# Seven half-size products for the last block's output projection, in a newly searched order

## The chip, the cores and the metric

The kernel runs on one core of one Trainium2 chip. Its engines work side by side, each through its own list of instructions in order: TensorE (PE, its weight loads shown as PEld), VectorE (DVE), ScalarE (ACT), GpSimd (POOL) and SyncE (SP). They wait for each other by semaphores. DMAs are issued here from POOL (loads, which also turn f32 into bf16) and from SP (stores and DMA transposes), and run on the same 16 DMA engines. The metric is the device time of one execution in microseconds, the median of several runs.

## The reference

```python
k_proj = np.einsum('ks,bhsd->bhkd', E, k)
v_proj = np.einsum('ks,bhsd->bhkd', F, v)
scores = scale * np.matmul(q, k_proj.transpose(0, 1, 3, 2))
attn = softmax(scores)                                   # over the 64 projected keys
x = np.matmul(attn, v_proj)   ->  x of 8192 tokens x 512
out = ((1 / (1 + np.exp(-(x @ w_gate)))) * (x @ w_val)) @ w_out
```

Eight batches, eight heads, 1024 positions, head size 64: attention against 64 projected keys, and then a gated feed-forward layer with d_model 512 and d_ff 1536. Inputs and output are f32; the kernel multiplies in bf16.

## The kernel before, in words

A batch gives two blocks of 512 tokens, so there are 16 blocks. For each batch, attention makes `xT` (x transposed, in bf16) for its two blocks: POOL loads K, V and Q in halves of four heads (512 KB each in SBUF); TensorE projects K and V (job `kv`); SP turns Q by DMA transposes (`turnq`, four per batch) and the projected K (`turnk`); TensorE makes the scores (`sc`), DVE the row maxima and their subtraction, ACT the exponentials; SP turns these (`turnp`); TensorE multiplies with V (`xo`); DVE inverts the sums, POOL or DVE divides; SP turns the result (`turnx`). K and V share SBUF with the exponentials and the quotients, so the loads of a batch wait until the previous one's `turnx` transposes have landed.

Then each block goes through the feed-forward layer. The gate product G and the value product V have a 2x2 split (half of the 512 inputs by half of the 1536 hidden units, two halves of the tokens) that is computed with seven half-size products instead of eight (`seven`, L1152). Sums of quarters are formed first: S1 = A21 + A22, S2 = S1 - A11, S3 = A11 - A21, S4 = A12 - S2 (`xs_sum`), and sums of the weights T1 to T4. The seven are A11·B11, A12·B21, S2·T2, S1·T1, S3·T3, A22·T4 and S4·B22. They accumulate in three PSUM banks a, c and f: ACT copies a to c after the first; copies a out ("snap") after S2·T2 and again after S3·T3; DVE adds a copy to f. One such product is four matmuls of 256 columns.

The output projection is done by `o_jobs` (L1369). For the first block and the last, it is plain (`o_plain`, L1309): for each of four tiles of 128 tokens, 12 matmuls of 512 columns into a bank, a copy by ACT and a store of 256 KB; in the last block the fourth tile is cut into two halves of 256 columns, with two stores of 128 KB. For the 14 blocks between, it is the same seven-product scheme, each product in two pieces j of six matmuls with 256 columns (0.65 us), with the sums S1 to S4 of the hidden units formed by `s_sum` (L1251; S4 on POOL in the middle blocks, where `AT["g4"]` is 1). There DVE merges f with a copy of a (`mergeO`), ACT copies c and a out (`leaveO`), and four stores follow.

All work outside the constants is cut into jobs, numbered in the order of their creation. `ORDER` (L159) lists these numbers in the order in which the instructions are put out; each engine takes its own of them in that order. A -1 stands for one fill product (`busy`, L720): a matmul of 256 columns with the unit matrix, whose result nobody reads. `PLACES` (L315) gives each job's PSUM bank or buffer. `Scheduler.job` (L350) takes a `release` argument and does not keep it.

Jobs that the texts speak of: 0 and 1, 6 and 7 are the products of the first K projection; 2, 3, 8, 9 copy it; 12, 14, 32, 34 transpose Q; 4 and 10 transpose K; 16, 22, 36, 42 are scores (17, 23, 37, 43 their maxima); 28, 30, 48, 50 transpose the exponentials; 52, 53, 59, 60 project V; 56, 63 make x; 112 to 163 are plain products of the first block, the first two of after's list being 119 and 113. Batch 1: 294 and 301 project K and V, 306 to 309 are its `turnq`. Batch 4: 1017 to 1020 load K and V, 1021 and 1022 Q, 1023 to 1026 are `turnq`, 1027 is `kv`, 1030 `turnk`. Batch 6: 1753 loads the first half of K, 1754 to 1756 the rest of K and V, 1763 is `kv`; 2014 to 2016 are S4 sums of an output block, 1904 and 1906 sums of x for S2 and S4. Near the end: 2850 is the last value product, 2851 its addition, 2820, 2847, 2849 and 2852 are gates, 2873 to 2882 belong to block 14's output, and 2887 on is the last block's output (before 15 jobs to 2901, in after 32 jobs to 2918: 2887 to 2892 the sums S1 to S3, 2893/2894 A11·B11, 2895 the bank copy, 2896/2897 A12·B21, 2898 S4, 2899 copy of c, 2900/2901 S2·T2, 2902 copy of a, 2903/2904 S1·T1, 2905/2906 A21·T3, 2907 copy, 2908 merge, 2909/2910 A22·T4, 2911 copy, 2912/2913 A12·B22, 2914 merge, 2915 to 2918 the stores).

Of the kernel before, what the change touches and what calls it, by code (L numbers as in the profile page):

```python
# [29 lines left out]
    s2=0, s3=0, s4=0, s5=0, s6=0, s7=0, o0p=1, o1p=0, o2p=0, o3p=1, x1=0, x2=0, x3=0, x4=1, g1=0, g2=0, g3=0,  # L30
# [123 lines left out]
class Job:  # L154
# [221 lines left out]
def bass_linformer_attn__then__ffn_glu_sigmoid_kernel(  # L376
# [20 lines left out]
    with contextlib.ExitStack() as es:  # L397
# [383 lines left out]


        def first_batch():
            K_AT, Q_AT = ((6.4, 8.05), (10.65, 12.0)), ((9.35, 13.4), (28.8, 30.1))
            V_AT = ((15.9, 15.9), (18.35, 19.45))
            ENGS = ("ACT", "DVE", "POOL")

# [1117 lines left out]
```

## Time and profile before

| | us |
|---|---|
| median of 3 runs (517.63 to 518.54) | 518.26 |
| the profiled execution's own time | 518.57 |
| its span, first to last instruction | 516.8 |
| TensorE busy | 510.5 (99%) |
| DVE busy | 436.6 (84%) |
| ACT busy | 374.4 (72%) |
| POOL busy | 169.8 (33%) |

The page cuts the span into 40 slices of 12.9 us: the busy digit of TensorE is 9 in all but the first and the last, and so is the granted clock in all. The 16 DMA engines are busy at nine tenths in the first five slices and move 138 GB/s on the mean. A group line gives an operation's shape, its count, the busy time and the mean of one. Matmuls are pipelined, so the time that one adds is the step from its start to that of the next, not its shown duration. "Idle before" and the waits name what ended an engine's wait.

### The profile page before, as it was taken

How to read it: one execution, taken by the hardware profiler on the slowest of the kernel's cores; microseconds unless marked ns; L12 is line 12 of the kernel's file. 1: busy time of each engine (PE TensorE's matmuls, PEld its weight loads, DVE VectorE, ACT ScalarE, POOL GpSimd, SP SyncE). 2: the span in 40 equal slices, each digit the busy share in tenths (PEclk: the TensorE clock that was granted, in tenths of full speed). 3: DMA queues.
4: the chain of work that ended last, by engine and by line, in shares of the span. 5: the costliest groups of instructions: out<-in, count | busy, mean ns of one | idle time of the engine just before them, and what ended most of it. 6: DMA issues, size and time to landing. Idle time of an engine off the chain costs nothing.

```text
span 516.8 us, 12171 instructions
## 1 busy us (share of the span) xinstructions
PE 510.5 (99%) x4741; PEld 426.6 (83%) x4741; DVE 436.6 (84%) x849; ACT 374.4 (72%) x714; POOL 169.8 (33%) x196
## 2 busy tenths in 40 slices
PE   8999999999999999999999999999999999999997
PEld 4555867889988899888998888888998889988884
DVE  6769998699988899869997799978989889968771
ACT  1566956888876796767867789777878679686652
POOL 9882004520435033340245113620053502403020
PEclk9999999999999999999999999999999999999999
DMA  9999938896679946995579957796545994530204
GB/s 159 198 198 207 181 70 175 136 201 124 148 148 170 188 92 128 155 179 115 119 143 174 158 103 128 156 196 113 142 98 129 202 169 104 96 90 1 82 2 162
DMA packets 140521, 71.57 MB, mean 138 GB/s; under 512 B 97200, under 2 KB 132272, under 8 KB 140464
## 3 DMA queue, kind: packets, MB, share of 16 engines
q1 hardware_dynamic: 104560, 40.91, 37.8%
q0 software_dynamic: 35904, 29.89, 37.8%
q8 instruction: 37, 0.61, 0.5%
q14 instruction: 20, 0.16, 0.1%
HBM read 60.29 MB, written 16.78 MB: 149 GB/s over the span
## 4 chain that ended last, share of the span: by engine, by line
PE 55%; DMA 3%; issue 1%; POOL 1%; ACT 0%; POOLq 0%
PE pF L518 28%; PE pA L518 27%; DMA KVs<-in_k_dram 3%; POOL KVs L559 0%; POOL Qb L559 0%; ACT ost L532 0%; POOL xS L547 0%; POOLq L129 0%
## 5 line engine op out<-in xcount | busy, mean ns | idle before, releaser
L532 ACT ACTIVATE spare<-pF 128x512 f32<-128x512 f32 (+2 forms) x167 | 94.2, 574 | 32.0 <-PE pF L518 22.7
L547 POOL TENSOR_TENSOR hT<-hT,hS 128x512 bf16<-128x512 bf16 x42 | 48.1, 1164 | 174.2 <-PE pA L518 96.8
L532 ACT ACTIVATE spare<-pA 128x512 f32<-128x512 f32 (+2 forms) x146 | 83.7, 586 | 20.2 <-PE pA L518 16.3
L1724 POOL TENSOR_TENSOR KVs<-spare,inv 128x384 bf16<-128x384 f32 (+1 forms) x41 | 29.6, 731 | 84.4 <-DVE topf L1635 35.3
L532 ACT ACTIVATE spare<-spare 128x512 f32<-128x512 f32 x74 | 46.1, 628 | 5.9 <-DVE spare L1146 5.5
L1146 DVE TENSOR_TENSOR spare<-pF,spare 128x512 f32<-128x512 f32 x59 | 40.1, 681 | 10.5 <-PE pF L518 5.2
L1215 DVE SCALAR_TENSOR_TENSOR hT<-spare,pF 128x512 bf16<-128x512 f32 x60 | 40.8, 679 | 7.7 <-PE pF L518 3.7
L518 PE MATMUL pA<-wO,hT 128*128 128x256 bf16 (+1 forms) x336 | 47.2, 280 | 0.0
L1146 DVE TENSOR_TENSOR spare<-pA,spare 128x512 f32<-128x512 f32 x54 | 36.7, 681 | 8.8 <-PE pA L518 6.4
L1215 DVE SCALAR_TENSOR_TENSOR hT<-spare,pA 128x512 bf16<-128x512 f32 x52 | 35.3, 678 | 8.3 <-PE pF L518 4.1
L518 PE MATMUL pF<-wO,hT 128*128 128x256 bf16 (+1 forms) x276 | 42.2, 296 | 0.0
L518 PE MATMUL pF<-xT,wV 128*128 128x256 bf16 (+1 forms) x248 | 39.9, 283 | 0.0
L518 PEld LDWEIGHTS pA<-wO,hT 128*128 128x128 bf16 x336 | 32.8, 98 | 6.5 <-ACT KVs L532 0.2
L518 PE MATMUL pA<-xS,wV 128*128 128x256 bf16 x248 | 37.2, 273 | 0.0
L518 PE MATMUL pA<-xT,wG 128*128 128x256 bf16 (+1 forms) x220 | 35.4, 284 | 0.6 <-DVE xT L876 0.5
L518 PE MATMUL pF<-xS,wG 128*128 128x256 bf16 x232 | 34.1, 272 | 0.0
L518 PEld LDWEIGHTS pF<-wO,hT 128*128 128x128 bf16 x276 | 26.6, 98 | 8.7
L518 PE MATMUL pF<-xS,tV 128*128 128x256 bf16 x224 | 33.6, 273 | 0.0
L518 PE MATMUL pA<-xS,tG 128*128 128x256 bf16 x208 | 31.2, 273 | 0.0
L518 PE MATMUL pF<-xT,wG 128*128 128x256 bf16 (+1 forms) x188 | 30.9, 286 | 0.0
L532 ACT ACTIVATE EF<-pA 128x512 f32<-128x512 f32 (+2 forms) x35 | 19.7, 564 | 14.4 <-PE pA L518 13.5
L518 PEld LDWEIGHTS pF<-xT,wV 128*128 128x128 bf16 x248 | 23.9, 98 | 4.3
(186 smaller groups left out, 1288.7 us busy)
## 6 DMA issues: line engine op xcount, KB each, us to landing
out_dram<-ost SPq DMA_DIRECT2D x63, 256.0 KB, 2.4
KVs<-in_v_dram POOLq DMA_DIRECT2D x15, 512.0 KB, 9.4
KVs<-in_k_dram POOLq DMA_DIRECT2D x14, 512.0 KB, 10.2
Qb<-in_q_dram POOLq DMA_DIRECT2D x14, 512.0 KB, 8.8
wO<-in_moe_w_out_dram POOLq DMA_DIRECT2D x1, 1536.0 KB, 28.1
wG<-in_moe_w_gate_dram POOLq DMA_DIRECT2D x5, 256.0 KB, 16.9
wV<-in_moe_w_val_dram POOLq DMA_DIRECT2D x5, 256.0 KB, 17.3
KVs<-in_k_dram POOLq DMA_DIRECT2D x4, 256.0 KB, 6.8
```

The lines of the kernel that those rows point to most:

```text
L518: lambda e: e.matmul(o, lhsT, rhs, **kw),
L532: lambda e: e.activation(o, i, func, scale=scale),
L547: fn = lambda e: e.tensor_tensor(o, a, b, op)
L1146: lambda e: e.tensor_tensor(PB(b)[:, :] if stay else BF(s), PB(b)[:, :], BF(s), ALU.add),
L1215: lambda e: e.scalar_tensor_tensor(o, y.rearrange("p (j c) -> p j c", j=2), 1.0, x.rearrange("p (j c) -> p j c", j=2), ALU.add, ALU.mult,),
L1724: fn = lambda e: e.tensor_tensor(xto.rearrange("p (g h d) -> p h g d", g=2, h=H)[:, hh[0] : hh[1], :, :], o[:, :, 0:DH].rearrange("p (h g) ...
```

## The change

`AT["o3p"]` goes from 1 to 0, so that `o_jobs` sends the last block through the seven-product scheme instead of `o_plain`. For that block all four sums are on DVE (`s_jobs` takes POOL only for blocks 1 to 14). `ORDER` and `PLACES` are new as a whole: all jobs are in a new order with new banks and buffers, and the list has 54 fill products instead of 35. The constants `K_AT`, `Q_AT`, `V_AT` and `LAND`, which go into `release`, are new. The order was searched with a longer share of the DMA engines given to the transposes. Everything else stays. Of the diff, the parts with the start, the loads and transposes of batch 4, batch 6's loads, and the end (in before's list, 1753 to 1757 stand together):

```diff
@@ -27,7 +27,7 @@
...
-    s2=0, s3=0, s4=0, s5=0, s6=0, s7=0, o0p=1, o1p=0, o2p=0, o3p=1, x1=0, x2=0, x3=0, x4=1, g1=0, g2=0, g3=0,
+    s2=0, s3=0, s4=0, s5=0, s6=0, s7=0, o0p=1, o1p=0, o2p=0, o3p=0, x1=0, x2=0, x3=0, x4=1, g1=0, g2=0, g3=0,
...
@@ -157,188 +157,189 @@
...
 ORDER = (
-    0, -1, -1, -1, 1, 2, -1, -1, -1, -1, -1, -1, 14, 3, -1, 4, 15, 12, 5, -1, 6, 13, -1, 16, 22, 17, -1, 7, 23,
-    18, 19, 8, -1, -1, -1, 24, 34, 9, 20, 25, -1, -1, 10, 32, 35, 11, 21, 33, 26, -1, -1, -1, -1, -1, -1, -1,
-    -1, -1, 36, 42, 28, 37, 52, 43, 38, 53, 39, 27, 44, 54, 29, -1, 30, 45, 40, 59, 55, 31, 46, -1, -1, -1, -1,
-    -1, 56, 41, 60, 57, 47, 48, 58, 169, 61, -1, -1, 50, 49, 119, 62, 168, 51, 112, 346, 63, 118, 174, 64, 65,
-    113, 124, 176, 128, 126, 125, 180, 130, 129, 127, 178, 114, 131, 115, 116, 165, 120, 68, 175, 122, 66, 121,
...
-    1267, 1188, 1242, 1176, 1269, 1189, 1243, 1178, 1022, 1099, 1191, 1179, 1282, 1036, 1100, 1192, 1182, 1190,
-    1252, 1246, 1019, 1271, 1183, 1194, 1247, 1167, 1020, 1241, 1195, 1255, 1244, 1018, 1193, 1256, 1169, 1198,
-    1017, 1253, 1199, 1258, 1177, 1259, 1248, 1180, 1262, 1026, 1254, 1203, 1276, 1196, 1204, 1025, 1184, 1263,
-    1181, 1205, 1197, 1257, 1206, 1283, 1249, 1219, 1260, 1284, 1277, 1185, 1220, 1200, 1245, 1278, 1207, 1201,
...
-    1421, 1217, 1027, 1231, 1422, 1261, 1410, 1024, 1213, 1228, 1288, 1502, 1028, 1229, 1423, 1029, 1425, 1506,
...
-    1976, 1989, 1757, 2005, 1913, 1992, 1756, 1835, 1978, 2011, 1994, 1916, 1979, 1754, 2018, 1820, 1990, 1753,
...
-    1951, 2022, 2142, 1962, 2238, 2143, 1904, 1952, 1937, 1906, 2144, 1961, 1963, 1938, 2024, 1905, 1966, 2157,
-    1967, 2145, 1933, 1763, 2146, 1953, 2025, 2240, 2158, 2242, 1954, 2026, 2159, 1764, 1964, 2148, 2030, 1765,
...
-    2832, 2808, 2845, 2868, 2833, 2783, 2843, 2801, 2863, 2846, 2810, 2871, 2772, 2865, 2867, 2827, 2848, 2864,
-    2850, 2849, 2869, 2787, 2866, 2812, 2870, 2830, 2872, 2788, 2831, 2834, 2795, 2813, 2873, 2798, 2874, 2847,
-    2811, 2851, 2875, 2816, 2799, 2814, 2877, 2876, 2818, 2815, 2802, 2880, 2817, 2878, 2803, 2881, 2835, 2879,
-    2819, 2893, 2804, 2883, 2836, 2882, 2884, 2820, 2885, 2886, 2852, 2887, 2890, 2888, 2894, 2896, 2891, 2892,
-    2899, 2889, 2897, 2898, 2895, 2900, 2901,
+    0, -1, -1, -1, -1, -1, -1, 1, 2, 3, -1, -1, -1, -1, -1, -1, -1, 12, -1, 4, 13, 14, 15, -1, -1, -1, 6, 5, -1,
+    22, 16, 23, -1, 7, 24, 8, 17, 9, -1, -1, -1, -1, 32, 34, 25, -1, 18, 33, 10, 26, 19, 35, 11, 20, -1, -1, -1,
+    -1, -1, -1, -1, -1, -1, -1, -1, -1, 42, 36, 52, 43, 27, -1, -1, 44, 45, 37, -1, -1, -1, 30, 21, -1, -1, -1,
+    38, 53, 39, 46, 28, 31, 59, 29, 54, 40, 55, -1, -1, -1, -1, -1, -1, -1, 56, 47, 60, 57, 41, 50, 58, 169, 61,
+    -1, -1, -1, 48, 51, 119, 168, 49, 62, 113, 63, 174, 118, 64, 65, 112, 346, 121, 128, 175, 120, 114, 176,
...
+    1246, 1020, 1099, 1179, 1164, 1251, 1190, 1192, 1018, 1182, 1247, 1282, 1019, 1252, 1194, 1084, 1253, 1017,
...
+    1280, 1193, 1199, 1259, 1248, 1257, 1022, 1249, 1262, 1278, 1196, 1177, 1219, 1263, 1207, 1180, 1220, 1200,
...
+    1406, 1214, 1228, 1216, 1215, 1407, 1217, 1409, 1231, 1421, 1027, 1222, 1026, 1422, 1410, 1213, 1025, 1229,
+    1285, 1028, 1286, 1029, 1288, 1501, 1408, 1030, 1423, 1502, 1289, 1232, 1169, 1031, 1290, 1425, 1023, 1412,
+    1218, 1503, 1411, 1413, 1233, 1294, 1426, 1024, 1506, 1416, 1234, 1428, 1417, 1505, 1291, 1032, 1414, 1427,
...
+    1943, 1996, 2014, 1941, 1944, 2008, 1984, 1942, 1927, 1755, 1985, 1946, 1928, 1906, 2000, 1947, 1929, 2001,
+    1986, 1955, 2015, 2017, 1950, 2002, 1956, 1930, 2007, 1945, 1753, 1931, 1957, 1948, 1951, 1757, 2141, 1917,
...
+    2024, 1963, 1905, 2021, 2025, 1953, 2022, 1964, 1936, 2026, 2143, 1965, 1966, 1763, 1937, 1967, 1759, 1997,
...
+    2772, 2846, 2801, 2827, 2856, 2812, 2787, 2863, 2813, 2788, 2795, 2866, 2848, 2830, 2811, 2798, 2834, 2865,
+    2868, 2814, 2799, 2849, 2831, 2816, 2864, 2869, 2867, 2817, 2871, 2835, 2870, 2872, 2847, 2818, 2888, 2802,
+    2819, 2873, 2890, 2874, 2815, 2850, 2803, 2875, 2893, 2836, 2876, 2877, 2804, 2851, 2880, 2820, 2894, 2887,
+    2881, 2895, 2852, 2878, 2892, 2889, 2896, 2879, 2882, 2900, 2891, 2885, 2901, 2884, 2903, 2883, 2902, 2886,
+    2905, 2906, 2897, 2907, 2904, 2898, 2909, 2908, 2910, 2912, 2911, 2913, 2899, 2915, 2916, 2914, 2917, 2918,
...
@@ -781,8 +782,8 @@
 
 
         def first_batch():
-            K_AT, Q_AT = ((6.4, 8.05), (10.65, 12.0)), ((9.35, 13.4), (28.8, 30.1))
-            V_AT = ((15.9, 15.9), (18.35, 19.45))
+            K_AT, Q_AT = ((7.05, 8.4), (11.1, 12.45)), ((9.8, 13.75), (29.1, 30.45))
+            V_AT = ((16.35, 16.35), (17.7, 20.3))
             ENGS = ("ACT", "DVE", "POOL")
 
             def step(name, key, n, body, keep, release=0.0):
@@ -1009,8 +1010,8 @@
             )
 
         LAND = {
-            "G": (20.1, 21.45, 26.1, 34.2, 23.5, 31.5, 36.85),
-            "V": (20.75, 22.15, 27.5, 35.5, 24.8, 32.9, 38.25),
+            "G": (20.5, 21.75, 26.4, 34.65, 23.75, 32.1, 37.3),
+            "V": (21.05, 22.45, 27.8, 36.0, 25.05, 33.35, 38.7),
         }
 
         def landed(n, j):
```

325 rows, old and new, of tables (ORDER, PLACES) are left out of this document.

## The prediction

> **What bounds the kernel now.** I read four views, in this order: the waits of TensorE, the busy time by stretch, the chain around the one long wait, and the timeline of both ends. The waits of TensorE (engine, line, releaser: total us, times, longest):
>
> ```profile
> PE pA L518 <- DMA KVs<-in_k_dram: 1.1, 2, 0.9
> PE pA L518 <- DVE tV L642: 1.1, 1, 1.1
> PE pA L518 <- DVE xT L876: 0.5, 1, 0.5
> ```
>
> Little else waits. The busy time by stretch (window: length, then PE, PEld, DVE, ACT, POOL busy, granted clock, DMA share, GB/s):
>
> ```profile
> 24.00:62.00 38.00, 37.34 (x300) 23.58 (x299) 32.41 (x63) 26.27 (x51) 16.63 (x17) 1.00 1.32 201
> 62.00:200.00 138.00, 138.00 (x1300) 116.96 (x1301) 122.88 (x241) 107.30 (x207) 41.33 (x48) 1.00 0.80 144
> 200.00:240.00 40.00, 39.12 (x361) 34.32 (x359) 33.54 (x61) 29.16 (x56) 13.16 (x15) 1.00 0.91 150
> 240.00:500.00 260.00, 260.00 (x2497) 229.98 (x2495) 223.79 (x424) 198.31 (x380) 77.65 (x85) 1.00 0.62 122
> ```
>
> TensorE is full outside three places: the start, 24 to 62 us and 200 to 240 us. So the time moves by TensorE work added or removed, by its few waits, and by the tail. The chain from 205 to 235 us (start, length, what) shows the long wait:
>
> ```profile
> 210.43 0.81 POOL Qb L559
> ...
> 212.36 2.25 POOL KVs L559 x3
> 214.61 16.57 DMA KVs<-in_k_dram
> 231.17 0.04 issue
> 231.22 1.99 PE pA L518 x16
> ```
>
> A half of K for batch 4 needs 16.57 us to land. The trace's landings show why: a half of Q was loaded first (landed 216.74), and two Q transposes ran through the four K and V loads, which landed 3.0 to 4.1 us apart (220.86, 224.85, 227.88, 231.17). One batch later, with no transpose among them, they landed 2.5 to 2.8 us apart. The timeline of the end (start, length, engine, line, out<-in):
>
> ```profile
> 503.56 5.34 PE L518 MATMUL pF<-wO,hT 128*128 128x512 bf16 x24
> 508.74 2.75 PE L518 MATMUL pA<-wO,hT 128*128 128x512 bf16 x12
> 511.33 1.47 PE L518 MATMUL pF<-wO,hT 128*128 128x256 bf16 x12
> 512.64 1.47 PE L518 MATMUL pA<-wO,hT 128*128 128x256 bf16 x12
> 514.15 0.38 ACT L532 ACTIVATE ost<-pA 128x256 f32<-128x256 f32 x1 [0.87 <-PE pA L518]
> 514.56 0.33 SPq L1360 DMA_DIRECT2D out_dram<-ost  x1
> ```
>
> The plain block runs without a gap; then one small copy and one half-size store remain (landed 516.30).
>
> **The change, part by part.** The sum is against the profiled execution: span 516.8, time 518.57, so 1.77 lies around the span. The median of the runs, 518.26, is 0.31 lower, and I carry the difference over to it.
>
> *Start.* The list of after has 54 fill products (-1) where before has 35, all ahead of the plain products. Fills here step by 0.109 us (nine from 15.05 take 1.0), so 19 more are 2.07 us. Part of it fills waits: by the step from each matmul to the next, before loses about 1.6 us between 7.5 and 22.2 us. I walked the new order by hand with durations of the timeline: score reduce or normalize on DVE 0.59 a step, sum with reciprocal 0.82, exp 0.60, a bank's turned copy 0.34 on DVE and 0.5 to 0.6 on ACT, 0.43 from a product's start to its reader. The loads of the start are issued as before, so they land as before (K 8.41, 11.10, 12.43). The first K product moves from 8.48 to 8.82, the last from 12.47 to 12.7, first scores of the second four heads from 16.16 to 16.27. DVE then has idle bits of 0.8 us that before hasn't, its last two normalizations end at 22.35 (before 21.6), and three fills stand between the last two transposes: the first plain product starts at 23.07, not 22.22. **+0.85**; from 0 (the fills replace waits only) to 2.07 (none hidden). I take the walk, whose durations are rows of this stretch.
>
> *22 to 62 us.* Before has small waits here: 0.34 in all at 22.4 to 24.3, 0.19 at 30.05 (Q landed 30.41), 0.25 at 34.4 (a gate weight landed 34.64) and, from step to step, 0.70 at 48.2 (the profile's 0.5, ended by DVE's copy of xT). In after's order the products that need those loads stand 1 to 5 us behind the landings, and a plain product and the V projection stand between the copy and the first products that need its sums. **-1.48**; 0 if equal waits come back. Batch 1's K is loaded before both Q halves (by the bytes ahead of it landing near 56.5, not 58.99); its Q transposes begin near 59.0 instead of 56.50, but its first scores come near 67, and need two that I expect by 65.6.
>
> *Batch 4.* The Q half that led is now behind the K and V loads, and the transposes stand behind the projection on SP. The loads should land near 226, the projection stands at 227 to 231. **-1.05** (the step from 230.06 is 1.156, an undisturbed one 0.107); between 0 and that.
>
> *Last block.* Plain: 503.56 to 513.95 (the last row plus twelve steps) is 10.39 us. Seven products of 12 matmuls, 84 by 0.1093 (that last dozen's step): 9.18. **-1.21**. Six sums by DVE for S1 to S3 (0.41 at 512 elements, 0.68 at 1024), one for S4 (near 0.95, extrapolated), two copies to spare, a bank copy and two merges are new. Most lie beside: after the last value product DVE still has a sum-and-gate tail of 3.6 us, but four pieces of block 14's products and both first pieces of A11 (0.655 each) cover it. Not covered: the copy of bank a between S2·T2 and A21·T3 takes 0.91 from the end of one to the start of the other (as 499.15 to 500.06), with one piece of 0.655 between: 0.25, and 0.05 for the sum S2 being just late. **+0.3** (0.25 if the sum is on time, 0.9 if DVE is one 0.6 step late).
>
> *Tail.* Before, from the last matmul's slot (513.95) to the landing: 0.2 + 0.38 copy + 0.03 + 1.74 = 2.35. After: 0.25, then the last merge on DVE 0.68, 0.03, one store issue of 0.40, then the second 256 KB store. SP issues them in order behind the other two, ready 1.4 us earlier, so these don't block. A lone store landed in 2.03 to 2.06, the fourth in a row in 2.56; two behind two is between, 2.25. Together 3.6: **+1.25** (1.0 to 1.6). The Trainium skill, DMA: Bandwidth & Descriptors, section "Anatomy of one DMA — SWDGE (gpsimd) path", fits a fixed 2.0 us plus bytes over 436 GB/s, for another issue path: an estimate of 2.6 us for the last store, and of 517.55 for the run. The trace's lone stores are faster.
>
> *New waits elsewhere.* Every other step is reordered too; counts of all other instructions stay. From 62 to 500 us before has one long wait, and otherwise about 0.3. Copy-to-product distances in after's list are as short as before's, but one is shorter: a sum, a gate and a bank copy ahead of a value product near 106 have about 0.3 us too little. The landing constants in the diff enter only an argument that Scheduler.job drops: no instruction. **+0.3** by the nearest row; below nothing only by the waits already taken out, and at most 2.6 if waits of before's size return.
>
> Sum: 0.85 - 1.48 - 1.05 - 1.21 + 0.3 + 1.25 + 0.3 = **-1.04**, so 517.2 against the median.
>
> **The rivals.**
> *The fills are not covered* (start +2.07): 517.2 + 1.22 = 518.4. For it: TensorE does 0.86 us more work in all. Against it: 1.6 us of waits at the start.
> *Transposes meet loads elsewhere*: 1.05 comes back, 518.25, at worst 519.2. For it: in batch 7 before already waits 0.15 at 425.8 on the K transpose, behind three Q transposes on SP, and after has 7.1 us of TensorE work from projection to score against 8.4. Against it: loads start earlier there. The Trainium skill, DMA: Bandwidth & Descriptors, "Queues, rings and completion order", says that each engine takes turns between the queues that have work; by that a transpose in flight slows every load, as the 3.0 to 4.1 us spacing above agrees.
> *Slower: batch 6's K half is late.* On POOL that load now stands behind two S4 sums and one x sum (1.16 to 1.39 each), with 7.4 us of TensorE work from its place to the projection. A load alone lands 5.6 us after issue, behind another 8.2. POOL waited 4.18 us for DVE before such an x sum at 350.61; if it does so here, the landing is 9.8 to 12.4 after the place, a wait of 2.4 to 5.0, and 519.6 to 522.2. It makes the kernel slower by 0.2% from a wait of 2.1 us on, that is 3.9 us of delay. Against it: the sums that it waits for stand 3.3 us ahead.
> *The start costs nothing* (fills only replace waits): 516.3.
>
> **How the numbers follow.** 0.2% (1.04 us) is about what a measurement can tell. Forecast 0.50, own range 516.4 to 518.0: it lies at the bound, and since the terms above it are waits seen and those below are priced by rows, I give 0.34 faster, 0.16 within. Fills 0.14 (0.12 within, 0.02 slower); transposes 0.14 (0.10 within, 0.04 slower); the late K half and its like 0.12, slower; the cheap start 0.10, faster. Faster 0.44, within 0.38, slower 0.18. The range 516.2 to 519.4 leaves out the worst of the late load and the best of the cheap start.
>
> **What would show it.** First plain product near 23.1; no wait near 48 and at batch 4's projection; the last product block near 9.5 us with one gap of 0.25 after S2·T2; 3.6 us from the last matmul to the last landing; 62 to 500 us full. It is wrong if a KVs or kpD landing ends a wait over 1 us, or the first plain product comes after 24.

## The result, and the profile after

The kernel became slower: 520.45 us (median of 9 runs, 519.93 to 523.05) against 518.26 (9 runs beside them), a ratio over all runs of 1.0051 with a 95% interval of 1.0036 to 1.0066 (the two medians alone give 1.0042). That is 1.9 to 3.4 us more, where the prediction had 1.0 less and its range ended at 519.4. The profiled execution took 520.57 with a span of 518.7, 2.00 more than the one of before (518.57).

The waits of TensorE, in the changed kernel (engine, line, releaser: total us, times, longest; line numbers are one higher than before):

```profile
PE pA L519 <- DVE tV L643: 1.1, 1, 1.1
PE pA L519 <- issue: 0.7, 1, 0.7
PE pF L519 <- DMA KVs<-in_k_dram: 0.4, 1, 0.4
PE pF L519 <- ACT pF L533: 0.3, 1, 0.3
PE pA L519 <- DMA Qb<-in_q_dram: 0.3, 1, 0.3
PE pF L519 <- ACT spare L533: 0.2, 1, 0.2
```

The 0.9 us of batch 4's K load and the 0.5 of the copy of xT, which the change was to remove, are gone. The other 0.2 of before's 1.1 for K loads belong to the first K load of the start, and are 0.4 now. Three new releasers stand in their place, and one wait of 0.7 with the releaser "issue", that is, none that the profile can name.

The busy time by stretch, changed kernel, same windows and columns as for before:

```profile
24.00:62.00 38.00, 37.34 (x305) 23.71 (x304) 31.31 (x62) 26.75 (x51) 17.24 (x18) 1.00 1.31 199
62.00:200.00 138.00, 137.11 (x1284) 115.54 (x1283) 121.89 (x235) 105.33 (x204) 41.35 (x48) 1.00 0.75 142
200.00:240.00 40.00, 40.00 (x374) 34.68 (x373) 34.00 (x66) 29.68 (x57) 13.38 (x16) 1.00 0.90 161
240.00:500.00 260.00, 260.00 (x2494) 229.48 (x2492) 226.43 (x428) 197.56 (x381) 76.51 (x85) 1.00 0.63 122
```

200 to 240 us is full now, as predicted. But 24 to 62 us has lost just as much as before (37.34 of 38.00 in both), and 62 to 200 us, which was full, has lost 0.9. The chain through the place where K was late for 1.05 us has no gap in it any more (start, length, what):

```profile
229.32 1.31 PE pF L519 x12
230.63 0.44 PE pA L519 x4
231.06 1.85 PE pF L519 x16
```

The timeline of the end (start, length, engine, line, out<-in):

```profile
512.95 1.47 PE L519 MATMUL pF<-wO,hT 128*128 128x256 bf16 x12
...
513.86 2.27 SPq L1303 DMA_DIRECT2D out_dram<-ost  x4
514.56 0.69 DVE L1405 SCALAR_TENSOR_TENSOR ost<-pF,spare 128x512 f32<-128x512 f32 x1 [1.75 <-PE pF L519]
```

The last slot of TensorE ends at 514.26, only 0.31 later than before. Then comes the merge on VectorE, which only begins when the last product is done, and two whole stores behind it, issued at 515.32 and 515.70; the last landed at 517.95, 3.69 us after the last slot, against 2.35 before.

Read matmul by matmul (the step from one to the next, less the usual step of its size), the places where TensorE lost over 0.15 us between 22 and 93 us are:

| before, at us | lost | changed, at us | lost | what ends it in the changed kernel |
|---|---|---|---|---|
| 22.0, 24.2 | 0.34 | 24.98 | 0.19 | no releaser named; before's at 24.2 is as long and stands at the same weight half |
| 30.05 | 0.19 | 29.05 | 0.46 | Q's third part, landed 29.67 |
| 34.4 | 0.25 | 56.48 | 0.50 | ScalarE's copy of a bank |
| 48.2 | 0.70 | 80.50 | 0.23 | ScalarE's copy out of a bank of products with V |
| | | 90.78 | 0.88 | the second transpose of the attention output, landed 91.69 |
| sum | 1.48 | sum | 2.26 | |

At 69.63 and 77.06 us the step is 0.22 too long as well, but no wait lies there: the trace lacks the record of a matmul. The weight loads go on at their usual step, the profile counts 312 weight loads and 310 matmuls with wO into pF, and early_after, mid_after and plain_end below, which have the same order there, show no such step. They also make some 0.1 of the 0.9 that the busy time lacks from 62 to 200 us. The recorded expectations below count them as waits: their 2.70 should be 2.26, and the price of the early order in them 0.80 + 0.78, or 1.6, and not 2.0.

The copy that ends the wait at 56.48 stands on ScalarE directly behind another operation that ended at 56.43 (start, length, engine, line, out<-in):

```profile
56.46 0.58 ACT L533 ACTIVATE pF<-pF 128x512 f32<-128x512 f32 x1
```

So most of the early waits went, but others came, and more of them.

### The profile page after: what moved, and what is told of

Same layout as the page of the kernel before. It is cut to its first block, busy times and chain, and to the rows that moved or that the text cites. A ratio compares the mean times of both kernels' runs of the same rounds, so it can differ in the third digit from the quotient of the medians.

```text
span 518.7 us, 12271 instructions
## 1 busy us (share of the span) xinstructions
PE 511.1 (99%) x4782; PEld 429.7 (83%) x4784; DVE 441.6 (85%) x858; ACT 372.8 (72%) x714; POOL 168.7 (33%) x196
## 4 chain that ended last, share of the span: by engine, by line
PE 90%; DMA 3%; DVE 3%; POOL 2%; issue 0%; ACT 0%; DVEq 0%; ACTq 0%; POOLq 0%
PE pA L519 45%; PE pF L519 45%; DMA Qb<-in_q_dram 3%; POOL KVs L560 1%; DVE topf L1636 1%; POOL wG L560 1%; POOL wV L560 1%; DVE pF L1663 0%; DVE pA L1663 0%; DVE hT L1216 0%; POOL Qb L560 0%; DVE hS L548 0%; ACT spare L533 0%; DVE ost L1405 0%; DVE hT L1057 0%
## 5 line engine op out<-in xcount | busy, mean ns | idle before, releaser
L533 ACT ACTIVATE spare<-pF 128x512 f32<-128x512 f32 (+2 forms) x152 | 86.1, 577 | 37.1 <-PE pF L519 27.1
L533 ACT ACTIVATE spare<-pA 128x512 f32<-128x512 f32 (+2 forms) x167 | 92.2, 572 | 27.3 <-PE pA L519 15.2
L1725 POOL TENSOR_TENSOR KVs<-spare,inv 128x384 bf16<-128x384 f32 (+1 forms) x52 | 37.5, 730 | 104.2 <-DVE topf L1636 36.4
L519 PE MATMUL pA<-wO,hT 128*128 128x256 bf16 (+1 forms) x276 | 37.9, 277 | 0.1
L519 PE MATMUL pA<-xT,wV 128*128 128x256 bf16 (+1 forms) x212 | 34.2, 285 | 0.0
L519 PE MATMUL pF<-xT,wV 128*128 128x256 bf16 (+1 forms) x196 | 32.0, 286 | 0.0
L519 PE MATMUL pF<-xS,wV 128*128 128x256 bf16 x208 | 31.0, 272 | 0.0
L519 PEld LDWEIGHTS pA<-wO,hT 128*128 128x128 bf16 x276 | 26.4, 98 | 4.4 <-ACT spare L533 0.2
L519 PE MATMUL pF<-wT,hT 128*128 128x256 bf16 x216 | 28.5, 273 | 0.2 <-ACT spare L533 0.2
L519 PE MATMUL pF<-xS,tV 128*128 128x256 bf16 x184 | 27.1, 273 | 0.0
```

The source lines that it names most:

```text
L519: lambda e: e.matmul(o, lhsT, rhs, **kw),
L533: lambda e: e.activation(o, i, func, scale=scale),
L1725: fn = lambda e: e.tensor_tensor(xto.rearrange("p (g h d) -> p h g d", g=2, h=H)[:, hh[0] : hh[1], :, :], o[:, :, 0:DH].rearrange("p (h g) ...
```

## The experiments

The change has four parts in time: the start to 23 us, the stretch to 93 us, the rest of the middle (batch 4 with it), and the last block. A given job number is the same job in both lists up to 2886, and at any time each list has at most 11 jobs behind it that the other has still ahead, so one can follow one list to a point and the other one from there on. In all kernels of this kind the banks and buffers of the second list are renamed where needed, so that none is held twice. Ratios are to the kernel before on the same chip; times worked out from them are on its 518.26. My theory after the traces was that the early order costs 2.0 (1.6 without the two missing records), batch 4 gains 1.05 and the last block loses 0.5 to 0.8; the rival, that the early order is worth what was predicted and the last block costs it all.

**Early order alone, and everything but it.**

```diff
 ORDER = (
-    0, -1, -1, -1, 1, 2, -1, -1, -1, -1, -1, -1, 14, 3, -1, 4, 15, 12, 5, -1, 6, 13, -1, 16, 22, 17, -1, 7, 23,
...
+    0, -1, -1, -1, -1, -1, -1, 1, 2, 3, -1, -1, -1, -1, -1, -1, -1, 12, -1, 4, 13, 14, 15, -1, -1, -1, 6, 5, -1,
...
+    519, 504, 435, 434, 556, 501, 436, 542, 502, 517,
     439, 520, 518, 437, 440, 522, 557, 505, 438, 400,
```

> The kernel before, with only its first 443 jobs (to about 93 us, the fills of the start included) in the order of the changed kernel; the rest, batch 4's loads and the plain last block too, in the old order. Theory (the lost time lies in the early order): the start costs 0.80 and the waits from 24 to 92 us are 2.70 against 1.48, so 518.26 + 2.0 = 520.3. Rival (the early order is worth what the prediction said, +0.85 - 1.48, and the loss comes from the end): 517.6.

Measured: 1.0037 (1.0023 to 1.0051), that is +1.9 us (1.2 to 2.6). The other half, against the changed kernel:

```diff
 ORDER = (
-    0, -1, -1, -1, -1, -1, -1, 1, 2, 3, -1, -1, -1, -1, -1, -1, -1, 12, -1, 4, 13, 14, 15, -1, -1, -1, 6, 5, -1,
...
+    0, -1, -1, -1, 1, 2, -1, -1, -1, -1, -1, -1, 14, 3, -1, 4, 15, 12, 5, -1, 6, 13, -1, 16, 22, 17, -1, 7, 23,
...
+    440, 522, 557, 505,
     523, 400, 506, 554, 399,
```

> The changed kernel with its first 458 jobs in the old order: the 35 fills and the stretch to about 93 us are those of the kernel before, all that follows is new, the seven products at the end too. Theory (early order): 520.45 - 2.0 = 518.4. Rival (loss at the end): 520.45 + 0.6 = 521.1.

Measured: 1.0004 (0.9995 to 1.0014), +0.2 (-0.3 to +0.7), 518.5 on the base of before. Both agree with the theory, with 1.6 as with 2.0 for the early order, and both exclude the rival: nearly all of what the whole change loses is in its first 93 us. The two make 2.1 together, inside the 1.9 to 3.4 of the whole.

**The start and the stretch behind it, apart.** Both lists have the same 61 jobs ahead of the first plain product, so they can be cut there.

```diff
 start_after:
...
+    -1, -1, -1, 48,
     49, 119, 62, 168, 51, 112, 346, 63, 118, 174, 64, 65,
 mid_after:
     61, -1, -1, 50,
+    51, 119, 168, 49, 62, 113, 63, 174, 118, 64, 65, 112, 346,
...
```

> The kernel before with only its first 61 jobs (all ahead of the first plain product) and the 54 fills in the new order. Theory (the prediction's walk): the first plain product starts 0.80 to 0.85 later and everything behind it too, 519.1. Rival (all 19 more fills count): 520.3. Rival (the later start only takes the place of the waits for loads at 24, 30 and 34 us, 0.78 in all): 518.3.

Measured: 1.0003 (0.9989 to 1.0017), +0.2 (-0.6 to +0.9). The interval has both the +0.85 of the walk and nothing; it excludes that all 19 fills count. In its profiled execution the first plain product stands at 23.26, 1.0 later than before's, and the waits from 22 to 62 us are 1.07 instead of 1.48: part of the later start is taken back because the loads are then there. That execution is among its longest (519.62): a sum on VectorE at 210.41 took 2.38 us instead of 0.68, beside a sum of GpSimd's, and TensorE lost 1.03 waiting for it at 211.71. I don't take more from it.

> The kernel before with its own start (35 fills, 61 jobs), then the jobs to about 93 us (the next 382) in the new order, then the old order again. Theory (the waits that went have come back as others): 2.70 against 1.48 between 22 and 93 us, +1.2, 519.5. Rival (the prediction's two terms, -1.48 and +0.3): 517.1.

Measured: 1.0017 (1.0002 to 1.0032), +0.9 (0.1 to 1.7). The prediction's two terms for this stretch (-1.48 and +0.3, 517.1) are excluded. With the start's +0.2 that makes 1.1, against 1.9 for the two together; the intervals cover the difference, and say no more of it. The waits of this kernel:

```profile
PE pA L517 <- DMA Qb<-in_q_dram: 0.9, 1, 0.9
PE pA L517 <- issue: 0.8, 1, 0.8
...
PE pF L517 <- ACT pF L531: 0.3, 1, 0.3
```

The reader is to see that the same three come back that the changed kernel has, at 28.28, 90.58 and 56.28 us. With the shorter start the first is larger (1.02 by the step): Q's third part landed at 29.47, and the new order has its product 1.0 us earlier than that.

**Batch 4 alone.**

```diff
-    1178, 1022, 1099, 1191,
+    1178, 1099, 1191,
...
-    1198, 1017, 1253,
+    1198, 1017, 1022, 1253,
...
-    1262, 1026, 1254, 1203, 1276, 1196, 1204, 1025, 1184,
+    1262, 1254, 1203, 1276, 1196, 1204, 1184,
...
-    1217, 1027, 1231,
+    1217, 1027, 1026, 1025, 1231,
```

> The kernel before with three jobs moved: batch 4's first half of Q is loaded behind its four K and V loads instead of ahead of them, and the two Q transposes stand behind the K projection instead of ahead of it. Theory: the wait of 1.05 (1.2 and 1.4 in two of the runs above) goes and nothing takes its place, 518.26 - 1.05 = 517.2. Rival (the Q transposes are then late for the first scores, or meet other loads): 518.3.

Measured: 0.9981 (0.9969 to 0.9993), -1.0 (-1.6 to -0.4), as predicted for this step. The four loads landed 2.5 to 3.2 us apart (216.78, 219.39, 221.93, 225.15), before 3.0 to 4.1 apart with the last at 231.17; the stretch by busy time is full:

```profile
200.00:240.00 40.00, 40.00 (x370) 34.66 (x369) 34.25 (x62) 29.56 (x56) 13.16 (x15) 1.00 0.93 152
```

**One early wait removed by hand.** At 48 us before waits for a copy on VectorE that stands behind two weight sums and a gate. Here it is put ahead of them.

```diff
-    187, 192, 109, 185, 302, 143, 198, 110, 214, 111, 199, 182,
+    187, 109, 111, 192, 185, 302, 143, 198, 110, 214, 199, 182,
```

> As the last one, and at 48 us the copy of the attention output (VectorE) stands directly behind the product that it reads, ahead of two weight sums and one gate that stood before it. Theory: the wait of 0.70 at 48.2 us goes as well, 516.5 to 516.7. Rival (the weight sums are now late for the first products that use them): 517.2.

Measured: 0.9979 (0.9969 to 0.9990), no different from the last one. The rival's time holds (no gain, 517.2), though what is late is a sum of x and not a weight sum; the timeline shows it (start, length, engine, line, out<-in, idle before and its releaser):

```profile
47.21 0.69 DVE L875 CAST xT<-pA 128x512 bf16<-128x512 f32 x1
...
48.31 1.04 PE L517 MATMUL pA<-xT,wG 128*128 128x256 bf16 x8
...
50.09 0.42 DVE L546 TENSOR_TENSOR xS<-xS,xT 128x512 bf16<-128x512 bf16 x1
...
50.56 0.61 PE L517 MATMUL pA<-xS,tG 128*128 128x256 bf16 x4 [0.79 <-DVE xS L546]
```

The copy ends 1.0 us earlier and its products run without a gap. One product group later TensorE waits 0.79 for a sum of the same x (a step 0.95 over the usual one), because VectorE, which is idle for under 0.2 us between 46 and 51 us, does the same work in another order. Here the wait for a full engine was not removed by letting its work change places; one such move was tried.

**The last block alone.**

```diff
     2774, 2679, 2673, 2677,
-    2680, 2748, 2854, ..., 2898, 2895, 2900, 2901,
+    2748, 2746, 2762, ..., 2914, 2917, 2918,
```

> The kernel before with only its last 180 jobs replaced: old order to about 480 us, then the new order with the last block in seven products. Theory: products -1.21, the gap for the bank copy +0.35, the tail from the last matmul to the landing +1.34: +0.5, 518.7; up to 519.0 when what lies behind the last landing is longer too. Rival (the end is what costs the 2.2): 520.4. Rival of the change's own: the products' saving is not eaten by the tail, 517.3.

Measured: 1.0010 (0.9998 to 1.0021), +0.5 (-0.1 to +1.1), as the theory has it and not clear of nothing; 520.4 and 517.3, the two rivals, are both out. The products pay 1.21, and the gap and the longer tail eat it.

```diff
-    2878, 2892, 2889, 2896, ..., 2913, 2899, 2915, 2916, 2914, 2917, 2918,
+    2878, 2879, 2882, 2885, 2884, 2883, 2886,
+    2893, 2887, 2890, 2888, 2894, 2896, 2891, 2892, 2899, 2889, 2897, 2898, 2895, 2900, 2901,
```

> The changed kernel with the last block's plain products put back at the end of its order (54 fills and all of the new order kept). Theory: 520.45 - 0.5 to 0.8, 519.65 to 519.95. Rival (the end costs the 2.2): 518.3. If the seven products do pay by themselves: 521.0 or more.

Measured: 1.0026 (1.0014 to 1.0039), so 519.6 on the base of before, as the theory has it. Some of the difference to the changed kernel is given away here: two pieces of A11 B11 stood among block 14's products; without them TensorE waits 0.42 at 501.5 and 0.15 at 502.6, where the changed kernel has no wait.

**The last block with a shorter tail.**

```diff
-    2892, 2889, 2896, 2879, 2882, 2900, 2891, 2885, 2901, 2884, 2903, 2883, 2902, 2886, 2905, 2906, 2897, 2907, 2904,
-    2898, 2909, 2908, 2910, 2912, 2911, 2913, 2899, 2915, 2916, 2914, 2917, 2918,
+    2889, 2892, 2900, 2879, 2882, 2901, 2891, 2885, 2884, 2883, 2886, 2902, 2896, 2903, 2905, 2906, 2907, 2897, 2904,
+    2899, 2920, 2921, 2898, 2908, 2909, 2910, 2912, 2911, 2913, 2915, 2916, 2914, 2917, 2919, 2918,
...
-            def merge(i, s, tok, col):
+            def merge(i, s, tok, col, js=slice(0, 2)):
...
-                            o,
-                            PB(f)[:, :].rearrange("p (j c) -> p j c", j=2),
+                            o[:, js],
+                            PB(f)[:, :].rearrange("p (j c) -> p j c", j=2)[:, js],
...
+            def half(tt, x):
...
+                    lambda e: e.dma_start(out_v[blk // 2, t][:, cc], ost[:, tt, cc]),
```

> The kernel before to about 480 us, then the new order with the seven products, and two things changed at its end: one more piece stands between S2 T2 and A21 T3, and the last merge and the last stores are halves (the left halves of the two last rows of tiles leave as soon as their copy is done; the right halves follow two merges of 128x256). Theory (it is the tail that eats the saving): products -1.21, gap 0.1, tail 2.8 against 2.35: about -0.5, 517.8. Rival (two stores at the end cost the same whether whole or half): 518.7 as with the end of the changed kernel.

Measured: 0.9986 (0.9978 to 0.9995), -0.7 (-1.1 to -0.3). The rival is out. The timeline of its end:

```profile
511.58 1.47 PE L518 MATMUL pA<-wO,hT 128*128 128x256 bf16 x12
...
512.48 0.81 SPq L1302 DMA_DIRECT2D out_dram<-ost  x2
513.19 0.89 DVE L1404 SCALAR_TENSOR_TENSOR ost<-pA,spare 128x256 f32<-128x256 f32 x2 [1.74 <-PE pA L518]
513.64 0.83 SPq L1451 DMA_DIRECT2D out_dram<-ost  x2
```

The last slot ends at 512.89, and the last half store, issued at 514.10, landed at 515.85: 2.96 us against the 3.69 of the changed kernel. The gap between S2 T2 and A21 T3 is gone, since one more piece stands in it; 0.21 at 504.7 is new. (A21 T3 is the product S3 T3 of the description: `s_sum` writes S3 in the place of A21, and S4 in that of A12.) So the 0.7 is the work of both edits, the piece in the gap and the halves, and the run does not part them.

**What holds up the transpose at 90 us.** The largest new wait has no releaser in the list; the timeline of the changed kernel shows what ended it:

```profile
91.78 0.60 PE L519 MATMUL pA<-xT,wG 128*128 128x256 bf16 x4 [0.72 <-issue]
91.78 0.43 DVE L548 TENSOR_TENSOR xS<-xT 128x512 bf16<-128x512 bf16 x1 [1.16 <-DMA xT<-KVs]
```

VectorE waits for the same tile in the same moment, and there the DMA is named: the transpose issued at 86.54 landed at 91.69, 5.15 us later, while the others of the four took 3.1 to 3.5. No load was in flight. The DMA view of 86 to 92 us has one line more than usual; changed kernel, then before (queue and kind: packets, MB, time of the packets as a share of 16 engines):

```profile
q1 hardware_dynamic: 2825, 0.92, 107.9%
q8 instruction: 1, 0.02, 1.3%
q14 instruction: 1, 0.01, 0.3%
```

```profile
q1 hardware_dynamic: 3054, 0.76, 63.2%
q8 instruction: 1, 0.02, 1.0%
```

Queue 8 carries packets of 16 KB, 38 in the changed kernel and 37 before, 623 and 606 KB; TensorE has 9566 and 9482 instructions, which comes to 65 and 64 bytes for each: so I take it for TensorE's program, fetched by some 256 instructions a time; in fetch_fills below, with 108 more instructions of TensorE ahead, it comes 5.7 us earlier, which bears that out. The packets of the transposes, 256 bytes each and at most 0.15 us from 80 to 83 us, took up to 1.47 us here. Before, such a fetch came at 88.65, when the second transpose was just landing. Two suspects, then: the fetch, or a store that the new order puts between the two transposes. Three kernels tell them apart.

```diff
 fetch_shift (warm-up products), and fetch_fills (the same with the fills):
-                mm(7, bank[7][:, :], warm[:, :], warm[:, :].unsqueeze(1).to_broadcast([P, 4, P]), ["warm"])
+                for x in range(4):
+                    mm(7, bank[7][:, x * P : (x + 1) * P], warm[:, :], warm[:, :], ["warm"], n=P)
 store_later (the store is job 431):
-    358, ..., 431, ..., 370, ..., 382,
+    358, ..., 370, ..., 382, 431,
```

> The changed kernel with its ten warm-up products of 128x512 written as forty of 128x128, the same columns in all: TensorE's program is 60 instructions further on at every later place, so each fetch of 16 KB of its program (256 instructions) comes about 3.3 us earlier against the work, and nothing else is changed. Theory (the fetch at 87.6 to 88.9 us holds up the second transpose of the attention output, which landed 5.15 us after its issue): the transpose lands in 3.1 to 3.5 and the wait of 0.88 at 90.8 us falls below 0.2, so about 0.7 less, 519.7. Rival (the store issued between the two transposes holds it up): the wait stays at 0.7 to 0.9, 520.4.

> The changed kernel with each of its 54 fill products of 128x256 written as two of 128x128: 108 more instructions of TensorE ahead of the plain products, the same columns. The fetch that stood at 87.6 to 88.9 should come some 5 us earlier, near 82, over transposes of the probabilities and not over the second transpose of the attention output. Theory (the fetch holds that transpose up): it lands 3.1 to 3.6 after its issue and the wait at 90.8 us is below 0.1. Rival (the store between the two transposes does): over 4.5, and the wait stays at 0.7 to 0.9. The time: 519.7 or 520.4, if the fills themselves take no longer.

> The changed kernel with one job moved: the store of 256 KB that stands between the first and the second transpose of the attention output (issued at 85.36) stands behind the third. Theory (fetch): the second transpose still takes over 4.5 and the wait at 90.8 stays at 0.7 to 0.9, 520.4. Rival (store): it lands in 3.1 to 3.6, the wait falls below 0.1, 519.7.

| kernel | fetch of TensorE's program, us | store between | second transpose, issue to landing | TensorE lost there |
|---|---|---|---|---|
| before | 88.65 to 89.59 | no | 85.60, 3.11 us | 0 |
| early_before | 88.52 to 89.53 | no | 85.39, 3.09 | 0 |
| start_after | 89.01 to 90.12 | no | 86.25, 3.12 | 0 |
| changed | 87.65 to 88.91 | yes | 86.54, 5.15 | 0.88 |
| early_after | 86.46 to 87.89 | yes | 86.27, 4.93 | 0.68 |
| mid_after | 89.08 to 90.76 | yes | 86.33, 5.20 | 0.94 |
| plain_end | 86.98 to 88.27 | yes | 85.94, 5.08 | 0.83 |
| fetch_shift | 86.09 to 87.04 | yes | 86.38, 4.49 | 0.24 |
| fetch_fills | 81.94 to 82.82 | yes | 86.45, 4.15 | 0 |
| store_later | 89.78 to 90.72 | no | 87.86, 5.66 | 1.40 |

Without the store the transpose took 5.66, so the store isn't it. In start_after and batch4_split a store lies beside the first and second transposes, and these took 3.1 to 3.4. With the fetch away the wait is gone, so the fetch is needed for it; the 4.15 that are left, over the 3.1 to 3.6 expected, come beside the store's last part and a packet of 8 KB of the same kind on queue 14 at 88.8, and stay open. One more thing is new in all kernels with the early order: the third transpose is issued while the second is in flight. Before, transposes that lay over each other so took 3.0 to 3.4, so that alone doesn't do it; that it adds to the fetch isn't excluded. Two reservations: the profiled execution of store_later is its longest (522.50, the others 520.13 to 520.76), with the first plain product at 24.82 and all behind it 1.3 to 1.8 us late, and the fetch lies over the transpose there all the same. And fetch_shift missed its aim: the fetch moved by 1.56 us against the changed kernel (by 0.37 against early_after, which has no more instructions), not 3.3, and still lay over the transpose, whose landing moved from 91.69 to 90.87; it took 4.49 where 3.1 to 3.5 was expected, the wait was 0.24 where under 0.2 was, and the first transpose, over which the fetch then lay too, took 4.58 (3.23 in the changed kernel). The DMA view of store_later, and of fetch_fills:

```profile
q1 hardware_dynamic: 2694, 0.67, 95.1%
q8 instruction: 1, 0.02, 1.0%
q14 instruction: 1, 0.01, 0.3%
```

```profile
q1 hardware_dynamic: 3360, 1.05, 78.5%
q14 instruction: 1, 0.01, 0.3%
```

With the fetch, 0.67 MB take more of the engines' time than 1.05 MB without it. The Trainium skill, DMA: Bandwidth & Descriptors, section "Queues, rings and completion order", says that each DMA engine takes turns between its queues by whole packets. By that, a packet of 16 KB in one turn would hold up the small ones by its own time, and packets of up to 1.47 us beside a fetch of 1.26 us are near that. But in store_later packets took up to 1.95 us beside a fetch of 0.94 us, and one of them began 0.2 us before the fetch and ended 0.8 after it. So that the transpose is held up beside the fetch is shown by these kernels, and how is not.

In time: fetch_shift 1.0030 (1.0018 to 1.0043), or 519.8, agrees with the 519.7 expected but does not exclude 520.4; fetch_fills 1.0051 (1.0037 to 1.0065), or 520.9, excludes 519.7; store_later 1.0043 (1.0028 to 1.0059), or 520.5, is as expected from the fetch. Moving a program against the work moves all its fetches: fetch_fills lost 0.88 less at 90.8 and 1.09 and 0.52 more at 136.4 and 276.9. The first of the two can be followed. TensorE waits there for a copy on ScalarE into a store's buffer:

```profile
136.89 0.60 ACT L532 ACTIVATE ost<-pA 128x512 f32<-128x512 f32 x1 [1.24 <-issue]
```

ScalarE waits for the store that was issued at 132.16. It landed at 136.81, 4.66 us later, where the same store of the changed kernel took 2.52 with no fetch near it; here a fetch of TensorE's program came at 135.00 to 135.92, and two transposes in flight beside it took 4.89 and 3.80 (3.08 and 3.06). So the fetch that was moved away from 88 us costs as much elsewhere, and the time did not fall. At 276.9, where the profile names a sum on GpSimd, a fetch at 267.48 to 269.39 lies over three stores that took 3.9 to 4.6 us (2.0 to 2.3 in the changed kernel); that this is the cause is not shown.

**Both gains in one kernel:** the diffs of batch4 and seven_split, the rest as before.

> The moves of batch4 and the end of seven_split in one kernel, the rest in the old order. The two are 270 us apart. Theory: the gains add, 0.9981 times 0.9986 is 0.9967, 516.5. Rival (what the one shifts brings other transposes under a fetch, and half of it is lost): 517.4.

Measured: 0.9973 (0.9962 to 0.9984), -1.4 (-2.0 to -0.8), 516.9 on the base of before (the median was 517.02, with 518.42 for the kernel before beside it). The expected 0.9967 lies inside, and so, just, does the rival's 0.9983. It is faster than both the kernel before and the changed one.

## Why the prediction was wrong

*Start, +0.85.* The walk gave 23.07 for the first plain product; in the profiled execution it came at 23.02. From one execution to the next it moves by more than that: in the eight profiled with the old start it stands at 21.64 to 22.49 (22.1 on the mean), in the changed kernel, early_after, plain_end and start_after at 22.86 to 23.25, and in store_later at 24.82. So about 0.9 holds, and the agreement to 0.05 is luck. By itself the new start costs +0.2 (-0.6 to +0.9) in the runs, which excludes neither the walk's value nor nothing.

*22 to 62 us, -1.48.* **This is the first step that failed.** Of the products that were to stand 1 to 5 us behind their loads, the one for Q's third part was due 0.4 us ahead of its landing (29.67; 29.09 in before, though the loads of the start were to land as before, and even with that it would have stood 0.2 behind). And the term counted only what goes. Three of the four groups of waits did go, and of the first a step of 0.19 stayed; with it, 1.15 us of waits stand in the same stretch, Q's third part with 0.46 and the copy at 56.48 with 0.50 the largest. I compared distances between a copy and its product in the list, and not the queue of ScalarE ahead of that copy, where a tanh ended at 56.43.

*New waits elsewhere, +0.3.* **The second, and of about the same size**: between 62 and 93 us they were 1.11, with 0.88 at one place, the transpose beside the fetch. The bound of 2.6 that stood beside the 0.3 was of the right size (1.15 and 1.11 are 2.26); taking the nearest row was the error. That row, a full stretch, belonged to an order in which the fetch at 88.65 came just as the second transpose was landing (88.71). Both terms together were -1.18; measured alone, in mid_after, +0.9 (0.1 to 1.7).

*Batch 4, -1.05.* Right: -1.0 (-1.6 to -0.4) alone, and no wait there in the changed kernel.

*Last block, -1.21 and +0.3.* Right: seven products, and one gap, of 0.35, after S2 T2.

*Tail, +1.25.* Right: 3.69 against 2.35, +1.34; the last whole store landed in 2.25, the value taken. The 2.6 that the prediction estimates from the Trainium skill, DMA: Bandwidth & Descriptors, section "Anatomy of one DMA — SWDGE (gpsimd) path", for another issue path, did not come. With the two steps before it +0.34 was predicted for the last block, and +0.5 (-0.1 to +1.1) measured.

In one sum for the two profiled executions, whose spans differ by 1.92 us and whose times by 2.00: 0.80 for the start, 1.02 more from the first plain product to 93 us (0.93 of it in the table above, as one wait of before's, 0.15, lies ahead of its first plain product), 0.12 from there to 200 us, -0.93 to 240 us, where batch 4 lies, 0.25 to 480 us, then -1.22 for fewer matmuls, 0.26 for waits behind 480 us (with the gap of 0.35), 1.34 for the tail, and 0.27 more from the last landing to the end of the span. They make 1.91. The 0.27 does not come from the new end, since end_after has 0.47 there and before 0.49.

Of the rivals three did not come: the fills were covered as far as the walk said, no K half was late in batch 6 (240 to 500 us is full), and no transpose was late beside loads. The fourth, a start that costs nothing, is not excluded by the runs. The signs asked for in the prediction were all there but the last, and its condition for being wrong (a landing of K or of kpD that ends a wait over 1 us, or a late start) named the wrong transfers.

## What to carry to other kernels

Price a reordering by what comes, not by what goes: where one engine was full here, a wait that was removed came back at another product, and a stretch that is full in the old order says little about the new one. A part of a reordered list can be tried by itself, by following one list to a point and the other from there; here that showed in two runs that a change sold as one had a loss of 1.9 early and a gain of 1.0 at one load. And at the end of a kernel it is the last result's way out that counts: seven products for eight did not pay with a whole merge and whole stores behind them (+0.5, -0.1 to +1.1), and gained 0.7 with halves and one more piece in the gap.

## What the hardware showed unexpectedly

TensorE's own program is a load like others: 16 KB for some 256 instructions, 7 to 20 us apart in the kernel before and the changed one, 0.9 to 2.0 us each. Over the 15 profiles of this study, kernels that are nearly the same, take the DMA transposes of 128x1024 with no load or store issued or in flight between their issue and their landing. Where no such fetch fell into the first 3.0 us (409 of them), they took 3.11 us in the median and 3.87 at most; where one did (154), 3.54 in the median and up to 5.14. Over 3.7 us were 3 of the first and 65 of the second. It matters when the fetch begins: where it began 1.0 to 2.0 us behind the issue, as with 1.1 in the changed kernel at 86.54, all 21 took over 3.7. A position in the program, which no list of jobs shows, so went with 0.4 us more of a transfer's time in the median and up to 2.0; what the fetch does inside the transfer is open.
